# Attention decode on one core: VectorE weights seven of V's eight chunks instead of five, a group's sum stands behind the next scores, and x and the biases come in one transfer

## The chip, the cores and the metric

The kernel runs on one core of a Trainium2 chip. The metric is device time in microseconds (us) of one execution; the number that counts is the median of repeated runs.

## The reference

Two blocks alternate, twice each, on one token of width 512. All numbers are 32-bit floats.

```
x = x + A(layernorm(x))      # A: q = x@wq, 32 heads; scores = q.k * 128**-0.5; softmax;
x = x + B(layernorm(x))      #    o = p.v; out = o@wo      (k_cache, v_cache: 32 heads x 4096 x 128)
x = x + A(layernorm(x))      # B: gelu(x@w1 + b1)@w2 + b2  (w1 512x1376, w2 1376x512)
x = x + B(layernorm(x))
```

The caches are 64 MB each and are needed by both A blocks, so nearly all the bytes that move are K and V, read twice. Nothing is large in arithmetic: one query row per head.

## The kernel before

**The work in groups.** The 32 heads form G = 8 groups of 4 heads (J = 4). A group's K and V are 8 MB each, laid out as 128 partitions x 16384 columns, in C = 8 chunks of NC = 2048 columns; its wq and wo slices are together 2 MB ("the pair", 128 x 4096). The first A block goes through groups 0 to 7, the second through 7 down to 0 (it keeps a little of group 6 and 7 on chip). Between them runs the MLP, block B, and at the end a second MLP.

**Memory.** One large tile, `arena`, holds three homes of 64 KB a partition (A, B, C) that K and V take in turns (`RING`, line 37; `homes`, line 514), and the small areas SHARED, SCRATCH and PAIR behind. K of group g+2 comes into the home of V of group g; V of g+1 into that of K of g. There is one PAIR area. PSUM tiles: `pS` takes the scores, and the next queries while no scores are there; `pO` takes V's weighted sums, output products and transposed weights.

**The order of transfers.** All large loads are issued from SyncE (SPq, line 107) in program order: K of a group, V of it, its pair, K of the next, and so on. An issue waits until its destination was read for the last time. The pair of a group waits for the output product of the group before it (that reads the wo half of PAIR, line 402); K and V behind it in the queue then follow at once.

**A group on the engines** (functions `group`, `partly`, `weighted`, `sum_up`, `head`, `out_product`, `next_queries`):

- TensorE: with the group's K there, 32 matmuls give the scores into `pS` (`scores`, line 223, 64 records in the trace). `exponentials` (line 228) takes the maximum on VectorE, exp on ScalarE. `weights` (line 241) turns the weights on TensorE, and copies them out of `pO` on VectorE (line 246): these are needed before anything is done with V.
- V's chunks are shared: BY_PE = 3 of the 8 chunks are weighted by TensorE (`values`, line 255), the other five by VectorE, in place: one multiply of 128 x 10240 (line 266), then three adds that halve what is left (line 271: 4096, 2048, 2048 columns).
- While VectorE does this, TensorE makes the next group's queries into `pS` from the wq half of the pair (`next_queries`, line 380). VectorE turns them (four transposes, line 170), makes `z` (line 219) and clears `pS` (line 385). The next scores need `z` and the cleared `pS`.
- `sum_up` (line 275) adds VectorE's chunk into `pO`, `head` (line 279) turns it and reduces it to the group's output column, and `out_product` (line 299) multiplies it with wo. Of this, `sum_up` and `head` stand ahead of the next group's scores, `out_product` stands behind them.

The last group of the first A block, the one before it, and the last group of the second block have all eight chunks weighted by TensorE; the first groups of the second block, taken from what was kept, too. So eleven groups use VectorE's way. In the last group of all, V comes in pieces (4, 2, 1, 1 chunks), behind it wo, w1 and w2 of the closing MLP; `idle` (line 187) issues matmuls into an unused PSUM range while V's last chunks are worked on.

**The start.** x, b1 and b2 come by three small transfers that ScalarE issues (lines 130 to 132).

Of the kernel before, what the change touches and what calls it, by code (L numbers as in the profile page):

```python
# [17 lines left out]
P = 128  # L18
# [4 lines left out]
J = 4  # L23
# [15 lines left out]
KEPT_V = 26 * U  # L39
SHARED = B_AT + KEPT_V  # L40
SCRATCH = SHARED + 10 * U
PAIR = SHARED + 11 * U
KEPT_K = PAIR + 2 * NC
TURNED = SHARED + 9 * U
ARENA = KEPT_K + 2 * U
HALVES = ((0, 4), (4, 8))
BY_PE = 3
ZQ = C - 1 + J * C
WIDE = 32 * J + 8 + 3 + 1
FRONT = 192  # L50
# [5 lines left out]


@with_exitstack
def decode_layers(ctx: ExitStack, tc: tile.TileContext, x, k, v, w, w1, b1, w2, b2, out):
    nc = tc.nc  # L60
    const = ctx.enter_context(tc.tile_pool(name="const", bufs=1))
    psum = ctx.enter_context(tc.tile_pool(name="psum", bufs=1, space=bass.MemoryType.PSUM))
# [19 lines left out]
    def small(name, n=1):  # L82
        nonlocal first_front, rest
        if name.startswith("gelu_"):
            i = "huaztg".index(name[-1])
            return cells[:, gelu + FB * i : gelu + FB * (i + 1)]
        if name not in places:
            fit = [j for j in range(J) if gaps[j] + n <= ends[j]]
            if name in ("b1c", "b2c", "xcol"):
                places[name] = front, first_front, n  # L90
                first_front += n
            elif fit:
                places[name] = cells, gaps[fit[0]], n
                gaps[fit[0]] += n
            else:
                places[name] = cells, rest, n
                rest += n
        t, a, m = places[name]
        assert m == n and first_front <= FRONT and rest <= CELLS
        return t[:, a : a + n]  # L100

    def at(first, n):
        return arena[:, first : first + n]
# [9 lines left out]
    def quarters(first):  # L113
        return [at(first + U * j, U) for j in range(4)]
# [4 lines left out]
    def of_w(row, i, n):  # L119
        return w[row][:, NC * i : NC * (i + n)]  # L120
# [5 lines left out]
    wq_t = by_four(load(SHARED, of_w(1, 0, 1)))  # L126
    nc.vector.memset(wide, 1.0)
    nc.vector.memset(cells[:, WIDE:], 0.0)
    b1c, b2c, xcol = small("b1c", FB), small("b2c", 4), small("xcol", 4)
    nc.scalar.dma_start(xcol, x)  # L130
    nc.scalar.dma_start(b1c, b1)
    nc.scalar.dma_start(b2c, b2)

    make_identity(nc, ident)
    negmean = small("negmean")
# [19 lines left out]
    def of_32(t, n, i=0):  # L155
        return t[:, : 32 * n].rearrange("p (c q) -> p c q", q=32)[:, :, i]
# [59 lines left out]
    def queries(src, negm, wide=False, to=None):  # L216
        qt = turned(src, wide, to)
        z = zq
        nc.vector.scalar_tensor_tensor(z[:, C - 1 :].rearrange("p (j n) -> p j n", j=J)[:, :, 0], of_32(qt, J, 1), negm, of_32(qt, J),
                                       op0=ALU.mult, op1=ALU.add)  # L220
        return z

    def scores(z, c, kt):
        for j in range(J):
            matmul(pS[32 * j : 32 * j + C, :], z[:, C * j + C - 1 - c : C * j + 2 * C - 1 - c], kt[j],
                   start=(c == 0), stop=(c == C - 1))
# [32 lines left out]

    def weighted(pt, home):
        first = home + NC * BY_PE
        t = at(first, NC * (C - BY_PE)).rearrange("p (n d) -> p n d", d=P)
        w = pt.rearrange("p c j b -> p (c j b)")[:, 4 * J * BY_PE :]
        nc.vector.tensor_tensor(t, t, w.unsqueeze(2).to_broadcast([P, 4 * J * (C - BY_PE), P]), op=ALU.mult)  # L266
        n = C - BY_PE
        while n > 1:
            m = n // 2
            a, b = at(first + NC * (n - 2 * m), NC * m), at(first + NC * (n - m), NC * m)  # L270
            nc.vector.tensor_tensor(a, a, b, op=ALU.add)  # L271
            n -= m
        return quarters(first)

    def sum_up(t):
        for j in range(J):
            matmul(pO[32 * j : 32 * j + 4, :], one.to_broadcast([P, 4]), t[j], start=False, stop=True)

    def head(rl, last=False):
        ot = at(SCRATCH, U)  # L280
        nc.vector.transpose(ot, pO)  # L281
        o, on = small("o", 4), on_wide
        own = at(SCRATCH, 4 * 129).rearrange("p (b q) -> p b q", q=129)[:, :, :P]
        own = own.rearrange("p b (d q) -> p d b q", q=32)[:, :, :, 0]
        nc.vector.tensor_reduce(o, own, axis=AX.X, op=ALU.add)
        if last:
            nc.vector.tensor_scalar(on[:, :4], o, rl, None, op0=ALU.mult)
        else:
            nc.vector.tensor_scalar(in_quarters(on, 4), o.unsqueeze(1).to_broadcast([P, J, 4]), rl, None,
                                    op0=ALU.mult)  # L290
        return on
# [7 lines left out]
    def out_product(on, wt, to, narrow=False):  # L299
        for d in range(4):  # L300
            if narrow:
                for j in range(J):
                    matmul(to[32 * j : 32 * j + 1, :P], on[:, d : d + 1], wt[:, d, P * j : P * (j + 1)],
                           start=(d == 0), stop=(d == 3))
            else:
                matmul(to, on[:, d : d + P], wt[:, d, :], start=(d == 0), stop=(d == 3))
# [73 lines left out]
    def next_queries(xs, negm, wt, to=pO):  # L380
        for c in range(4):
            wide_query_block(to, c, xs, wt)
        z = queries(to, negm, wide=True)
        if to is pS:
            nc.vector.memset(pS, 0.0)  # L385
        return z

    def add_up(acc, own):
        t = small("acc", 4)
        nc.vector.scalar_tensor_tensor(t, own, 1.0, acc, op0=ALU.mult, op1=ALU.add)  # L390
        return t


    def group(z, acc, ahead, k_blocks):
        if ahead:
            t, rl, wt = ahead
            sum_up(t)
            on = head(rl)
        for c, t in k_blocks:
            scores(z, c, t)  # L400
        if ahead:
            out_product(on, wt, pO)
        p = exponentials(sc, nsc)
        if ahead:
            acc = add_up(acc, of_32(turned(pO, wide=True), 4))
        return acc, *weights(p)

    def partly(pt, v_blocks, home):
        for c, t in v_blocks:
            if c < BY_PE:  # L410
                values(c, pt, t, c)
        return weighted(pt, home)


    negm, z, sc, nsc = first_queries(xs, s, wq_t, wide=True)
# [2 lines left out]
    for g in range(G):  # L418
        final = g == G - 1
        k_home, v_home = RING[2 * g % 3], RING[(2 * g + 1) % 3]  # L420
        acc, pt, rl = group(z, acc, ahead, blocks(k, g, k_home, HALVES if final else ((0, C),)))
        ahead = None
        if g == G - 2:
            nc.scalar.copy(at(KEPT_K, 2 * U), at(k_home + NC * C - 2 * U, 2 * U))
        if g < G - 2:
            t = partly(pt, blocks(v, g, v_home), v_home)
            pair = load(PAIR, of_w(g % 2, g, 2))
            ahead = t, rl, by_four(pair[:, :NC])
            z = next_queries(xs, negm, by_four(pair[:, NC:]), to=pS)
            continue  # L430
        for c, t in blocks(v, g, v_home, LAST if final else ((0, C),)):
            values(c, pt, t, c)
            if final and c in (5, 7):
                idle(pS)
            if g == G - 2:
                for j in range(J):
                    i = 4 * c + j - KEPT_V // U
                    if i >= 0:
                        nc.scalar.copy(pK[i], t[j])
        if final:  # L440
            wo_t = by_four(load(PAIR, of_w(g % 2, g, 1)))
# [73 lines left out]
    for n in range(2, G):  # L515
        g, final = G - 1 - n, n == G - 1
        k_home, v_home = homes[(2 * n - 1) % 3], homes[2 * n % 3]
        acc, pt, rl = group(z, acc, ahead, blocks(k, g, k_home, HALVES if final else ((0, C),)))
        if not final:
            t = partly(pt, blocks(v, g, v_home, ((0, 6), (6, 8)) if n == 2 else ((0, C),)), v_home)  # L520
            pair = load(PAIR, of_w(g % 2, g - 1, 2))
            ahead = t, rl, by_four(pair[:, NC:])
            z = next_queries(xs, negm, by_four(pair[:, :NC]), to=pS)
            continue
        for c, t in blocks(v, g, v_home, LAST):
            values(c, pt, t, c)
            if c in (5, 7):
                idle(pS)
        wo_t = by_four(load(PAIR, of_w(g % 2, g, 1)))
        for a, b in W1_AT_END:  # L530
            load_w1(A_AT, a, b)
        for a, b in W2_AT_END:
            load_w2(A_AT + 11 * U, a, b)
        own = head_out(rl, wo_t, last=True)
# [47 lines left out]
```

## Time and profile before

| | |
|---|---|
| median of 3 runs | 673.45 us (673.1 to 673.54) |
| profiled execution, its own time | 673.82 us |
| its span (first to last instruction) | 672.0 us |
| TensorE matmul busy | 395.3 us (59%) |
| VectorE busy | 329.0 us (49%) |
| ScalarE, GpSimd busy | 22.8 us, 4.8 us |
| moved | 285.98 MB, 426 GB/s over the span |
| mean granted TensorE clock | 0.790 of full speed |

The profile gives busy times by engine, a strip of 40 slices over the span, the DMA queues, the chain of waits that ended last, and groups of instructions by line and form. A row of the timeline reads: start, duration, engine, line, operation, what it writes <- what it reads, form, count, and in brackets how long the engine was idle before it and what released it. "SPq" rows are SyncE's issues. A float matmul leaves two records, so 32 matmuls of scores are "x64". In the timeline of a later kernel the lines are that kernel's own; the added lines move them by 1 to 8.

### The profile page before, as it was taken

The page shows a single profiled execution, that of the slowest core. Times are in us where ns is not written, and L with a number is a line of the kernel's source. Part 1 is how long each engine was busy: PE and PEld are TensorE (multiplying, and loading weights), DVE is VectorE, ACT ScalarE, POOL GpSimd, SP SyncE. Part 2 cuts the span into 40 slices and gives each one's busy share as a digit, 9 for nine tenths or more (in the row PEclk, how much of TensorE's full clock was granted, in tenths as well). Part 3 has the DMA queues.
Part 4 walks back from the last instruction along what each step waited for, and adds up shares of the span by engine and source line. Part 5 has one row for each costly group of instructions (what it writes and reads, how often), then busy time and mean ns, then how long its engine had stood idle before and what let it go on. Part 6 is the DMA issues. An engine that isn't in the chain of part 4 may idle for free. (4 is left out here: it accounts for less than half of the span.)

```text
span 672.0 us, 5795 instructions
## 1 busy us (share of the span) xinstructions
PE 395.3 (59%) x2470; PEld 109.1 (16%) x2470; DVE 329.0 (49%) x480; ACT 22.8 (3%) x48; POOL 4.8 (1%) x23
## 2 busy tenths in 40 slices
PE   4533853647628456276777878728526566275586
PEld 1100210111102111011213222102101111021122
DVE  2049186293682845921112221492772936918522
ACT  0010000000000000011000110000000000000000
POOL 0000000000000000000000000000000000000000
PEclk9667775876768857787979999877759767677688
DMA  9999999999999999999999999999999999999996
GB/s 375 437 434 437 437 438 433 405 465 434 437 437 401 447 430 426 437 438 422 437 410 403 412 447 427 429 445 430 433 437 408 459 437 431 437 433 413 433 416 278
DMA packets 11545, 285.98 MB, mean 426 GB/s; under 512 B 1792, under 2 KB 1792, under 8 KB 3584
## 3 DMA queue, kind: packets, MB, share of 16 engines
q1 hardware_dynamic: 11088, 285.61, 99.0%
q8 instruction: 19, 0.31, 0.2%
q10 hardware_dynamic: 432, 0.01, 0.0%
q14 instruction: 6, 0.05, 0.0%
HBM read 285.62 MB, written 0.00 MB: 425 GB/s over the span
## 5 line engine op out<-in xcount | busy, mean ns | idle before, releaser
L111 PE MATMUL pO<-arena,cells 128*128 128x512 f32 (+4 forms) x376 | 92.9, 605 | 143.9 <-DVE arena L271 126.9
L111 PE MATMUL pS<-arena,front 128*8 128x512 f32 x1036 | 144.7, 699 | 34.8 <-DMA arena<-in_k 31.0
L266 DVE TENSOR_TENSOR arena<-arena 128x10240 f32<-128x10240 f32 x11 | 119.1, 10826 | 33.1 <-DMA arena<-in_v 30.2
L111 PE MATMUL pO<-arena 128*4 128x512 f32 x584 | 92.1, 786 | 45.8 <-DMA arena<-in_v 43.9
L271 DVE TENSOR_TENSOR arena<-arena 128x2048 f32<-128x2048 f32 (+1 forms) x33 | 98.5, 2985 | 0.7
L229 DVE TENSOR_REDUCE cells<-pS 128x1 f32<-128x512 f32 x16 | 11.1, 692 | 152.3 <-PE pS L111 152.3
L111 PEld LDWEIGHTS pO<-arena,cells 128*128 128x128 f32 (+3 forms) x376 | 28.2, 123 | 193.5 <-DVE arena L271 136.0
L111 PE MATMUL pS<-arena,cells 128*1 128x128 f32 (+1 forms) x328 | 50.0, 381 | 12.7 <-DMA arena<-in_w 10.1
L111 PEld LDWEIGHTS pS<-arena,front 128*8 128x8 f32 x1036 | 31.2, 101 | 154.3 <-issue 118.0
L281 DVE STREAM_TRANSPOSE arena<-pO 128x512 f32<-128x512 f32 x16 | 11.5, 717 | 55.1 <-PE pO L111 55.1
L243 PE MATMUL pO<-front,arena 128*128 128x128 f32 x64 | 12.3, 323 | 36.6 <-ACT arena L238 36.6
L111 PEld LDWEIGHTS pO<-arena 128*4 128x4 f32 x584 | 16.2, 101 | 108.2 <-issue 104.2
L170 DVE STREAM_TRANSPOSE arena<-pO 32x128 f32<-32x128 f32 x64 | 19.9, 311 | 20.0 <-PE pO L111 19.0
L111 PEld LDWEIGHTS pS<-arena,cells 128*1 128x1 f32 (+1 forms) x328 | 22.0, 117 | 46.8 <-issue 36.2
L238 ACT ACTIVATE arena<-pS,cells 128x512 f32<-128x512 f32 x16 | 12.4, 778 | 502.3 <-DVE cells L234 502.3
L232 DVE TENSOR_REDUCE cells<-cells 128x1 f32<-128x8 f32 x16 | 2.6, 161 | 29.4 <-PE pO L111 29.2
L243 PEld LDWEIGHTS pO<-front,arena 128*128 128x128 f32 x64 | 7.6, 155 | 49.7 <-ACT arena L238 48.5
L170 DVE STREAM_TRANSPOSE arena<-pS 32x128 f32<-32x128 f32 x44 | 13.7, 311 | 0.8
L172 DVE STREAM_TRANSPOSE arena<-pS 128x128 f32<-128x128 f32 x3 | 1.0, 317 | 12.1 <-PE pS L111 12.1
L248 DVE STREAM_TRANSPOSE cells<-cells 128x32 f32<-128x32 f32 x16 | 3.4, 214 | 6.7 <-ACT arena L238 5.5
L385 DVE MEMSET pS<- 128x512 f32 x11 | 5.3, 485 | 1.2
L111 PE MATMUL pO<-arena,front 128*128 128x128 f32 (+2 forms) x18 | 5.1, 385 | 0.0
(63 smaller groups left out, 72.9 us busy)
## 6 DMA issues: line engine op xcount, KB each, us to landing
arena<-in_w SPq DMA_DIRECT2D x13, 2048.0 KB, 11.4
arena<-in_k SPq DMA_DIRECT2D x4, 4096.0 KB, 25.0
arena<-in_v SPq DMA_DIRECT2D x2, 4096.0 KB, 38.9
arena<-in_w SPq DMA_DIRECT2D x6, 1024.0 KB, 20.1
arena<-in_v SPq DMA_DIRECT2D x3, 2048.0 KB, 42.6
arena<-in_v SPq DMA_DIRECT2D x1, 6144.0 KB, 30.3
arena<-in_w SPq DMA_DIRECT2D x6, 688.0 KB, 30.7
arena<-in_v SPq DMA_DIRECT2D x4, 1024.0 KB, 46.2
```

The source lines that it names most:

```text
L111: tc.keep_in_program_order(nc.tensor.matmul(*a, **kw))
L170: nc.vector.transpose(t[q], src[q, P * j : P * (j + 1)])
L172: nc.vector.transpose(t, src[:, :P])
L229: nc.vector.tensor_reduce(ml[:, 0:1], pS, axis=AX.X, op=ALU.max)
L232: nc.vector.tensor_reduce(m, mt[:, :C], axis=AX.X, op=ALU.max)
L238: nc.scalar.activation(p, pS, AF.Exp, bias=bias[:, 0:1], scale=sc, accum_out=ml[:, 0:1])
L243: tc.keep_in_program_order(nc.tensor.transpose(pT[:, b].rearrange("p j r -> p (j r)"), p[:, P * b : P * (b + 1)], ident))
L248: nc.vector.transpose(lt, ml)
L266: nc.vector.tensor_tensor(t, t, w.unsqueeze(2).to_broadcast([P, 4 * J * (C - BY_PE), P]), op=ALU.mult)
L271: nc.vector.tensor_tensor(a, a, b, op=ALU.add)
L281: nc.vector.transpose(ot, pO)
L385: nc.vector.memset(pS, 0.0)
```

## The change

Four edits are made.

1. BY_PE goes from 3 to 1: TensorE weights one of V's chunks, VectorE seven. The multiply is split into chunks 1 to 3 (128 x 6144) and 4 to 7 (128 x 8192), and the adds are of 6144, 4096 and 2048 columns.
2. The call that makes the next queries stands between the two multiplies (`between`), with the load of the pair ahead of it in the same function. The turned queries get an area of their own.
3. In `group`, the scores come first; `sum_up`, `head` and `out_product` of the group before come behind them, the latter two behind the maximum in `exponentials`. `head` gets an area of its own (TURNED_HEAD).
4. x, b1 and b2 are one array and one transfer of 128 x 19.

```diff
-BY_PE = 3
+BY_PE = 1
...
-    b1c, b2c, xcol = small("b1c", FB), small("b2c", 4), small("xcol", 4)
-    nc.scalar.dma_start(xcol, x)
-    nc.scalar.dma_start(b1c, b1)
-    nc.scalar.dma_start(b2c, b2)
+    by_dma = small("by_dma", FB + 8)
+    b1c, b2c, xcol = by_dma[:, :FB], by_dma[:, FB : FB + 4], by_dma[:, FB + 4 :]
+    nc.scalar.dma_start(by_dma, vectors)
...
-    def weighted(pt, home):
-        first = home + NC * BY_PE
-        t = at(first, NC * (C - BY_PE)).rearrange("p (n d) -> p n d", d=P)
-        w = pt.rearrange("p c j b -> p (c j b)")[:, 4 * J * BY_PE :]
-        nc.vector.tensor_tensor(t, t, w.unsqueeze(2).to_broadcast([P, 4 * J * (C - BY_PE), P]), op=ALU.mult)
-        n = C - BY_PE
+    def weighted(pt, home, between):
+        w = pt.rearrange("p c j b -> p (c j b)")
+
+        def times(a, b):
+            t = at(home + NC * a, NC * (b - a)).rearrange("p (n d) -> p n d", d=P)
+            q = w[:, 4 * J * a : 4 * J * b]
+            nc.vector.tensor_tensor(t, t, q.unsqueeze(2).to_broadcast([P, 4 * J * (b - a), P]), op=ALU.mult)
+
+        times(BY_PE, C // 2)
+        z = between()
+        times(C // 2, C)
+        first, n = home + NC * BY_PE, C - BY_PE
...
-        return quarters(first)
+        return quarters(first), z
...
     def group(z, acc, ahead, k_blocks):
+        for c, t in k_blocks:
+            scores(z, c, t)
         if ahead:
             t, rl, wt = ahead
             sum_up(t)
-            on = head(rl)
-        for c, t in k_blocks:
-            scores(z, c, t)
-        if ahead:
-            out_product(on, wt, pO)
         p = exponentials(sc, nsc)
         if ahead:
+            out_product(head(rl, to=TURNED_HEAD), wt, pO)
             acc = add_up(acc, of_32(turned(pO, wide=True), 4))
         return acc, *weights(p)
...
+            def queries_here():
+                load(PAIR, of_w(g % 2, g, 2))
+                return next_queries(xs, negm, by_four(at(PAIR + NC, NC)), to=pS)
+
+            t, z = partly(pt, blocks(v, g, v_home), v_home, queries_here)
+            ahead = t, rl, by_four(at(PAIR, NC))
```

On VectorE, from the multiply of V to the next group's maximum, for the last group that VectorE weights (line 266 is the multiply, 271 the adds, 170 the query transposes, 219 `z`, 385 the clearing of `pS`, 281 to 289 `head`, 229 the maximum), before:

```order
L266 TENSOR_TENSOR arena<-arena 128x10240
L271 TENSOR_TENSOR arena<-arena 128x4096
L170 STREAM_TRANSPOSE arena<-pS 32x128
L271 TENSOR_TENSOR arena<-arena 128x2048
L170 STREAM_TRANSPOSE arena<-pS 32x128
L271 TENSOR_TENSOR arena<-arena 128x2048
L170 STREAM_TRANSPOSE arena<-pS 32x128 x2
L219 SCALAR_TENSOR_TENSOR front<-arena,cells 128x4
L385 MEMSET pS 128x512
L281 STREAM_TRANSPOSE arena<-pO 128x512
L285 TENSOR_REDUCE cells<-arena 128x4
L289 TENSOR_SCALAR cells<-cells 128x4x4
```

and at the same place now (268 are the multiplies, 277 the adds, 391 the clearing, 229 and 231 the maximum and its turn, 287 the start of `head`):

```order
L268 TENSOR_TENSOR arena<-arena 128x6144
L268 TENSOR_TENSOR arena<-arena 128x8192
L170 STREAM_TRANSPOSE arena<-pS 32x128 x4
L277 TENSOR_TENSOR arena<-arena 128x6144
L219 SCALAR_TENSOR_TENSOR front<-arena,cells 128x4
L391 MEMSET pS 128x512
L277 TENSOR_TENSOR arena<-arena 128x4096
L277 TENSOR_TENSOR arena<-arena 128x2048
L229 TENSOR_REDUCE cells<-pS 128x1
L231 STREAM_TRANSPOSE cells<-cells 128x32
L287 STREAM_TRANSPOSE arena<-pO 128x512
```

The query transposes stand behind both multiplies (not between them, as the source is written), and `z` and the clearing stand behind the first and largest add. `head` moved from ahead of the maximum to behind it.

On TensorE, from V's chunks of that group to the turned weights of the last group (`pO<-arena 4x512` are V's chunks, `pS<-arena,cells 128x512` the next queries, `pO<-arena,cells 4x512` is `sum_up`, `pS<-arena,front 8x512` the scores, `pO<-arena,cells 128x512` the output product, line 243 the turned weights), before:

```order
L111 MATMUL pO<-arena 4x512 x12
L111 MATMUL pS<-arena,cells 128x512 x4
L111 MATMUL pO<-arena,cells 4x512 x4
L111 MATMUL pS<-arena,front 8x512 x32
L111 MATMUL pO<-arena,cells 128x512 x4
L243 MATMUL pO<-front,arena 128x128 x4
```

and now:

```order
L112 MATMUL pO<-arena 4x512 x4
L112 MATMUL pS<-arena,cells 128x512 x4
L112 MATMUL pS<-arena,front 8x512 x32
L112 MATMUL pO<-arena,cells 4x512 x4
L112 MATMUL pO<-arena,cells 128x512 x4
L243 MATMUL pO<-front,arena 128x128 x4
```

`sum_up` went from ahead of the scores to behind them; the output product directly follows it there. SyncE's order of transfers is the same in both.

More of the change, by code (lines that the diff above doesn't have):

```diff
@@ L41 @@
 SCRATCH = SHARED + 10 * U
+TURNED_HEAD = SHARED + 8 * U
 PAIR = SHARED + 11 * U
@@ L58, in decode_layers @@
 @with_exitstack
-def decode_layers(ctx: ExitStack, tc: tile.TileContext, x, k, v, w, w1, b1, w2, b2, out):
+def decode_layers(ctx: ExitStack, tc: tile.TileContext, vectors, k, v, w, w1, w2, out):
     nc = tc.nc
@@ L88, in small @@
             fit = [j for j in range(J) if gaps[j] + n <= ends[j]]
-            if name in ("b1c", "b2c", "xcol"):
+            if name == "by_dma":
                 places[name] = front, first_front, n
@@ L277, in sum_up, with head @@
             matmul(pO[32 * j : 32 * j + 4, :], one.to_broadcast([P, 4]), t[j], start=False, stop=True)
-    def head(rl, last=False):
-        ot = at(SCRATCH, U)
+    def head(rl, last=False, to=SCRATCH):
+        ot = at(to, U)
         nc.vector.transpose(ot, pO)
         o, on = small("o", 4), on_wide
-        own = at(SCRATCH, 4 * 129).rearrange("p (b q) -> p b q", q=129)[:, :, :P]
+        own = at(to, 4 * 129).rearrange("p (b q) -> p b q", q=129)[:, :, :P]
         own = own.rearrange("p b (d q) -> p d b q", q=32)[:, :, :, 0]
@@ L382, in next_queries @@
             wide_query_block(to, c, xs, wt)
-        z = queries(to, negm, wide=True)
+        z = queries(to, negm, wide=True, to=at(TURNED + P, P) if to is pS else None)
         if to is pS:
@@ L397, in group, with partly @@
             sum_up(t)
-            on = head(rl)
-        for c, t in k_blocks:
-            scores(z, c, t)
-        if ahead:
-            out_product(on, wt, pO)
         p = exponentials(sc, nsc)
         if ahead:
+            out_product(head(rl, to=TURNED_HEAD), wt, pO)
             acc = add_up(acc, of_32(turned(pO, wide=True), 4))
         return acc, *weights(p)
-    def partly(pt, v_blocks, home):
+    def partly(pt, v_blocks, home, between):
         for c, t in v_blocks:
@@ L411, in partly @@
                 values(c, pt, t, c)
-        return weighted(pt, home)
+        return weighted(pt, home, between)
     negm, z, sc, nsc = first_queries(xs, s, wq_t, wide=True)
@@ L425, in decode_layers @@
         if g < G - 2:
[L426 to L429, printed above, removed]
+            def queries_here():
[3 more added lines that the diff above has]
+            ahead = t, rl, by_four(at(PAIR, NC))
             continue
@@ L519, in decode_layers, with queries_here @@
         if not final:
[L520 to L523, printed above, removed]
+            def queries_here():
+                load(PAIR, of_w(g % 2, g - 1, 2))
+                return next_queries(xs, negm, by_four(at(PAIR, NC)), to=pS)
+            t, z = partly(pt, blocks(v, g, v_home, ((0, 6), (6, 8)) if n == 2 else ((0, C),)), v_home,
+                          queries_here)
+            ahead = t, rl, by_four(at(PAIR + NC, NC))
             continue
@@ L561 @@
     arrays = dict(
-        x=columns(a["x"])[:, :, 0],
+        vectors=np.concatenate((b1.reshape(J, FB, 32).transpose(0, 2, 1).reshape(P, FB),
+                                columns(a["b2"])[:, :, 0], columns(a["x"])[:, :, 0]), axis=1),
         k=apart(a["k"].reshape(G, J, C, U, DH).transpose(0, 4, 2, 1, 3).reshape(G, P, BLOCK)),
@@ L566 @@
         w1=columns(a["w1"]).reshape(P, 4 * J * FJ),
-        b1=b1.reshape(J, FB, 32).transpose(0, 2, 1).reshape(P, FB),
         w2=w2.reshape(J, FB, 32, D).transpose(0, 2, 1, 3).reshape(P, FB * D),
-        b2=columns(a["b2"])[:, :, 0],
     )
```

## Prediction

> **What bounds the kernel now.** I read the page first, then the busy time by stretch, the chain of waits, and the timeline of one middle group and of the last one.
>
> ```profile
> span 672.0 us, 5795 instructions
> q1 hardware_dynamic: 11088, 285.61, 99.0%
> q10 hardware_dynamic: 432, 0.01, 0.0%
> ```
>
> The big transfers (q1) take 99.0% of the time of all 16 DMA engines. In stretches:
>
> ```profile
> 1.00:666.30 665.30, 392.42 (x2414) 107.18 (x2414) 328.38 (x478) 22.84 (x48) 4.44 (x18) 0.79 1.00 430
> 89.80:112.00 22.20, 9.91 (x40) 2.24 (x40) 21.56 (x10) 0.00 (x0) 0.00 (x0) 0.73 1.06 456
> ```
>
> The columns are the stretch, its length, busy time of TensorE, weight loads, VectorE, ScalarE, GpSimd, the granted clock, the DMA share and GB/s. From 1 us to 666.3 us the DMA share is 1.00: no engine of the 16 has a gap worth naming. Where VectorE is busy throughout (21.56 of 22.20 us) the transfers are no slower. So compute is free as long as it gives buffers back in time, and it counts at the very end. The chain of waits says the same:
>
> ```profile
> 604.64 42.62 DMA arena<-in_v
> ...
> 647.32 18.94 DMA arena<-in_w
> ...
> 666.30 2.93 PE pS L111 x56
> ```
>
> The last w2 piece that TensorE waits for lands at 666.26 us; behind it is a tail of 5.7 us. Two questions follow: does the change ever let the queue run dry, and does it push the last group's compute beyond 666.3 us?
>
> **Transfers and the start.** Bytes on the big queue are the same. The three small transfers became one; q10, which carries them, rounds to 0.0% of the span, under 0.05% or 0.34 us, and two of three of its packets go: I take a gain of 0.2 us (ends 0 and 0.34). An x that lands earlier or later changes nothing, since the queue is full then.
>
> **Middle groups: does the queue run dry?** A middle group, from scores to V to the next scores, and the shortest issue-to-landing of the page:
>
> ```profile
> 113.95 8.58 PE L111 MATMUL pS<-arena,front 128*8 128x512 f32 x64 [1.90 <-DMA arena<-in_k]
> 122.46 3.70 PE L111 MATMUL pO<-arena,cells 128*128 128x512 f32 x8
> 126.19 0.33 SPq L107 DMA_DIRECT2D arena<-in_w  x1
> 133.22 10.83 DVE L266 TENSOR_TENSOR arena<-arena 128x10240 f32<-128x10240 f32 x1 [3.68 <-DMA arena<-in_v]
> 157.41 9.04 PE L111 MATMUL pS<-arena,front 128*8 128x512 f32 x64 [1.90 <-DMA arena<-in_k]
> out<-cells SPq DMA_DIRECT2D x1, 2.0 KB, 1.4
> ```
>
> The pair is issued when the output product is done (126.19), 3.66 us behind the end T of the scores (122.53). V, the only thing then left in the queue, is used at 133.22: the queue has 7.0 us in hand. VectorE gets V at 133.22 and the next scores start when K lands, 24.19 us later (157.41).
>
> VectorE's new work until the scores may start: from the multiply of 10240 columns (10.82 us) and the add of 4096 (4.42 us, quoted below) one column costs 1.042 ns and an instruction 0.16 us. So 6144 columns take 6.56 us, 8192 take 8.69. Multiplies 6.56 + 8.69, four transposes 1.29, add 6.56, `z` 0.23, clearing 0.48, and some 0.2 between them: 24.0 us. That is 0.2 us ahead of K: the scores start as before. The other adds (4.42 + 2.29) end at 30.9 us, the scores not before 24.2 + 8.5: `sum_up` finds them done.
>
> Behind T a chain is longer now. Rows for its parts, from the last group and two other places:
>
> ```profile
> 638.58 3.70 PE L111 MATMUL pO<-arena,cells 128*128 128x512 f32 x8
> 638.73 0.69 DVE L229 TENSOR_REDUCE cells<-pS 128x1 f32<-128x512 f32 x1 [6.48 <-PE pS L111]
> 639.45 0.21 DVE L231 STREAM_TRANSPOSE cells<-cells 128x32 f32<-128x32 f32 x1
> 631.05 0.72 DVE L281 STREAM_TRANSPOSE arena<-pO 128x512 f32<-128x512 f32 x1 [0.50 <-PE pO L111]
> 632.01 0.23 DVE L289 TENSOR_SCALAR cells<-cells 128x16 f32<-128x16 f32 x1
> 321.61 1.29 DVE L170 STREAM_TRANSPOSE arena<-pO 32x128 f32<-32x128 f32 x4 [3.79 <-PE pO L111]
> 644.41 0.66 PE L243 MATMUL pO<-front,arena 128*128 128x128 f32 x4 [2.13 <-ACT arena L238]
> 645.29 0.29 DVE L246 COPY arena<-pO 128x128 f32<-128x128 f32 x1
> 382.32 7.05 PE L111 MATMUL pO<-arena 128*4 128x512 f32 x64 [0.41 <-DVE arena L246]
> ```
>
> `sum_up` is 8 records; at full clock 64 take 7.05 us, so about 1.0 us, beside VectorE's maximum and its turn (T + 1.0). Then `head`, 1.19 us from 631.05 to 632.24, with two small operations between its parts (0.4): T + 2.65. The output product starts at T + 2.7 and ends at T + 6.4, where it was T + 3.66: the pair is issued 2.75 us later. Of 7.0 us in hand 4.3 are left; 1.4 us from issue to landing (for a small transfer on an idle queue) is my bound for what it needs, so nothing runs dry. The weights of V are ready at: T + 6.4, transposes 1.3 and 0.1, turned weights 0.66 beside five small VectorE steps (1.05), copy 0.29, in all T + 9.2; in the middle group 113.95 + 8.58 + 9.2 = 131.7, ahead of V at 133.2. So the middle costs nothing. The 88 matmuls fewer on TensorE are hidden as well.
>
> **The last group.** Here K waits for compute, not the other way round:
>
> ```profile
> 608.67 10.82 DVE L266 TENSOR_TENSOR arena<-arena 128x10240 f32<-128x10240 f32 x1 [2.40 <-DMA arena<-in_v]
> 619.53 4.42 DVE L271 TENSOR_TENSOR arena<-arena 128x4096 f32<-128x4096 f32 x1
> 626.72 2.29 DVE L271 TENSOR_TENSOR arena<-arena 128x2048 f32<-128x2048 f32 x1
> 630.06 0.48 DVE L385 MEMSET pS<- 128x512 f32 x1
> 630.73 7.92 PE L111 MATMUL pS<-arena,front 128*8 128x512 f32 x64
> 645.64 7.03 PE L111 MATMUL pO<-arena 128*4 128x512 f32 x48 [0.57 <-DVE arena L246]
> 655.62 0.72 DVE L281 STREAM_TRANSPOSE arena<-pO 128x512 f32<-128x512 f32 x1 [9.97 <-PE pO L111]
> 661.26 0.76 PE L111 MATMUL pO<-arena,cells 128*2 128x344 f32 x8 [0.41 <-DMA arena<-in_w]
> 664.24 1.05 PE L111 MATMUL pS<-arena,cells 128*1 128x128 f32 x32 [1.15 <-DVE cells L334]
> ```
>
> Now the scores start at 608.67 + 24.03 + 0.05 = 632.75 instead of 630.73. They took 7.92 us because `sum_up` just ahead of them (from 629.07) had used up part of the slow clock; now they start from rest. Two rows give the ends for that:
>
> ```profile
> 288.12 8.54 PE L111 MATMUL pS<-arena,front 128*8 128x512 f32 x64 [1.90 <-DMA arena<-in_k]
> 244.44 9.89 PE L111 MATMUL pS<-arena,front 128*8 128x512 f32 x64 [1.92 <-DMA arena<-in_k]
> ```
>
> I take 9.2, the middle. T = 641.95, V's weights are used at T + 9.23 = 651.2 instead of 645.64. From there to `head` it took 9.98 us, of which 1.7 are lost to a half clock:
>
> ```profile
> 642.74:646.15 3.41, 1.17 (x12) 0.61 (x16) 2.52 (x12) 0.87 (x2) 0.00 (x0) 1.00 0.98 420
> 646.15:649.56 3.41, 3.41 (x24) 0.69 (x20) 0.00 (x0) 0.00 (x0) 0.00 (x0) 0.50 1.00 420
> 663.21:666.63 3.42, 1.38 (x44) 1.04 (x48) 0.56 (x4) 0.21 (x1) 0.00 (x0) 1.00 0.87 350
> 666.63:670.04 3.41, 2.58 (x52) 1.60 (x40) 0.48 (x2) 0.00 (x0) 0.00 (x0) 0.50 0.07 28
> ```
>
> The clock is granted in windows of 3.41 us. A window in which TensorE was busy 1.17 us (34%) or 1.38 us (40%) is followed by one at 0.50. In the changed kernel the rest between the output product and V's chunks is T + 6.4 to T + 9.2, with 0.66 us of work in it: a window that holds all of it (starting at T + 5.8 to T + 6.4) is at most 1.26 us busy (37%), and with 0.1 us to either side still 40%. That is 0.8 of 3.41 us of possible starts, and where the windows lie I can't say. So about three times in four the clock stays: 9.98 − 1.7 = 8.3 us, and `head` starts at 659.5 instead of 655.62, 3.85 us later.
>
> The MLP behind waited 0.41 us for w1 (661.26) and 1.02 us for w2 (664.24 + 1.05 to 666.30); both have landed by then. So w2's matmuls start at 659.5 + (664.24 − 655.62) − 0.41 = 667.7. Before, 56 of their 88 records ran mostly at half clock (2.93 us); now TensorE has no long rest ahead of them, and 88 records take, at 32 in 1.05 us, 2.6 us: 670.25 instead of 669.23. **Sum:** +1.0 − 0.2 = +0.8 us. On the profiled execution's own 673.82 us that is 674.6; the median of the runs lies 0.37 lower: 674.2.
>
> The Trainium skill, "TensorE: Matmul & The Clock Gate", Part 1 and its section on HAM oscillation, has the clock fall after an idle window of about 3.4 us and asks for no rest longer than that. By that rule the rest of 2.8 us would never cost anything and the sum would stay at +0.8. The trace differs: the window from 642.74 was 34% busy, and the clock still fell. So the fall stays a case here, and by the page's word that the windows run free of the program, its phase isn't to be had from this trace.
>
> **Rivals.** (1) *The clock falls in the last group* (slower). A late window of clock also makes the scores long (9.6 to 9.9 us) and puts the next window's start on the rest: +0.4 to +0.7 from the scores, +1.7 from V's chunks, on top of +0.8: about 676.6. It decides when the window starts 5.7 to 6.5 us behind T. For it: it happened in the profiled execution, 646.15. Against: the rest is shorter now.
> (2) *The pair comes too late, and the queue runs dry* (slower). Price: what the delay exceeds 2.75 us by, less the margin of 4.3 − 1.4 = 2.9 us, ten times. It needs the output product at half clock (+3.7): then 0.8 us a pair, more where the scores are long, 8 to 12 us, 682 to 686. Against: TensorE rests only 1.7 us ahead of it, half of a window.
> (3) *The last group hides it all*: scores at 8.5 us or `z` a little earlier, and 0.4 more of slack: 673.3, the small transfers' 0.2 us less.
> (4) *Faster*: all of the last group's delay is hidden and the w2 tail, 2.93 us, runs at full clock (some 1.2 us less): 672.0. It needs `head` before 657, 2.5 us earlier than worked out.
>
> **How the numbers follow.** About 0.2% (1.35 us: below 672.1, above 674.8) is what a measurement of this kernel can tell from no change. Forecast +0.8 with its own ends of the scores (8.54 to 9.89: 673.5 to 674.9): 0.58. Rival 1: 0.22. Rival 2: 0.06. Rival 3: 0.10. Rival 4: 0.04. Slower is rivals 1 and 2 and a seventh of the forecast's own range, 0.36; faster 0.04; same the rest, 0.60. The range from 672.9 to 677.2 takes in rival 3 and rival 1 and leaves out rivals 2 and 4 and an edge.
>
> **What would show it.** In the changed profile: DMA share 1.00 until 666 us, the pair issued some 6.4 us behind the end of the scores, K and not VectorE releasing the scores in the middle groups, the last scores at about 632.7 and released by VectorE's clearing, V's last chunks from 651, and no wait for w2 in the tail. I am wrong if a DMA dip stands at each pair, if the multiplies take longer than their columns, or if the last group's scores start by 631.

## The result and the profile after

The changed kernel takes 682.09 us (median of 6 runs, 680.29 to 685.54); the kernel before took 673.5 us on the same chip (6 runs, 673.1 to 673.84). The ratio is 1.0133, 95% interval [1.0115, 1.0151]: 8.6 us slower. The forecast of 674.2 us and its range up to 677.2 are missed. What happened is what rival 2 names, the pair that comes too late; it had 0.06. The runs also spread over 5 us where the kernel before spreads over less than 1. The profiled execution took 683.58 us, its span 681.8 us, 9.8 us more than before.

The page of the changed kernel, span and big queue:

```profile
span 681.8 us, 5432 instructions
q1 hardware_dynamic: 11088, 285.61, 98.1%
```

Packets and bytes are those of before; their time is 98.1% of the span, not 99.0%, so transfers have gaps now. And 98.1% of 681.8 us is 668.8 us, where 99.0% of 672.0 was 665.3: the same packets also took some 3.5 us longer. Where, the busy time by stretch shows; first before (last number: GB/s):

```profile
1.00:660.00 659.00, 388.70 (x2356) 105.86 (x2356) 326.63 (x470) 22.63 (x47) 3.90 (x17) 0.79 1.00 430
100.00:300.00 200.00, 109.25 (x544) 27.72 (x544) 119.70 (x131) 4.52 (x9) 0.00 (x0) 0.74 1.00 432
300.00:320.00 20.00, 12.20 (x74) 3.24 (x74) 4.08 (x17) 4.05 (x8) 0.00 (x0) 0.83 0.98 424
320.00:380.00 60.00, 46.65 (x476) 15.81 (x478) 12.48 (x57) 1.25 (x4) 2.27 (x9) 0.94 0.99 411
470.00:490.00 20.00, 10.06 (x38) 2.61 (x36) 15.61 (x16) 0.87 (x2) 0.00 (x0) 0.81 1.00 430
490.00:640.00 150.00, 84.10 (x424) 21.23 (x425) 90.67 (x101) 2.60 (x6) 0.00 (x0) 0.73 1.00 432
```

and the same stretches now:

```profile
1.00:660.00 659.00, 361.58 (x2068) 105.30 (x2072) 414.76 (x471) 22.62 (x47) 3.69 (x16) 0.77 0.99 424
100.00:300.00 200.00, 98.67 (x474) 27.27 (x472) 158.91 (x131) 4.52 (x9) 0.00 (x0) 0.73 1.00 430
300.00:320.00 20.00, 14.42 (x80) 3.71 (x76) 4.77 (x20) 4.05 (x8) 0.00 (x0) 0.83 0.94 391
320.00:380.00 60.00, 45.88 (x438) 15.47 (x442) 11.52 (x55) 1.08 (x3) 2.27 (x9) 0.94 0.98 403
470.00:490.00 20.00, 12.99 (x80) 3.74 (x70) 9.94 (x20) 0.87 (x2) 0.00 (x0) 0.93 0.79 325
490.00:640.00 150.00, 70.38 (x308) 20.50 (x307) 122.05 (x99) 2.60 (x6) 0.00 (x0) 0.72 1.00 428
```

As an estimate, a stretch loses its length times (1 − GB/s now / GB/s before). Up to 660 us: 659 x (1 − 424/430) = 9.2 us, nearly all of the 9.8. By place: 0.9 us over the four pairs up to 300, 1.6 at the pair of 305, 1.2 in the MLP, 4.9 between 470 and 490, 1.4 over the three pairs behind (a GB/s is rounded, and a packet counts in the stretch in which it starts, so each is good to about half a us).

A middle group of the changed kernel, the one whose rows the prediction shows of before:

```profile
113.39 8.89 PE L112 MATMUL pS<-arena,front 128*8 128x512 f32 x64 [12.69 <-DMA arena<-in_k]
122.10 1.04 PE L112 MATMUL pO<-arena,cells 128*4 128x512 f32 x8
124.47 3.70 PE L112 MATMUL pO<-arena,cells 128*128 128x512 f32 x8 [1.33 <-DVE cells L295]
128.20 0.33 SPq L108 DMA_DIRECT2D arena<-in_w  x1
132.68 15.16 DVE L268 TENSOR_TENSOR arena<-arena 128x6144 f32<-128x6144 f32 x2 [2.00 <-DMA arena<-in_v]
```

K still releases the scores. Behind their end (122.28) come `sum_up`, `head`, the output product, and 5.92 us behind it the pair, where it was 3.66: 2.3 us later. From the pair's issue to the use of V are 4.5 us, where there were 7.0. This distance is called the pair's lead below.

The group with the large loss is the first of the second block that VectorE weights. The timeline of VectorE, then of TensorE and SyncE, and behind it two stretches of 2 us:

```profile
438.22 15.16 DVE L268 TENSOR_TENSOR arena<-arena 128x6144 f32<-128x6144 f32 x2
453.42 6.56 DVE L277 TENSOR_TENSOR arena<-arena 128x6144 f32<-128x6144 f32 x1
459.89 1.28 DVE L170 STREAM_TRANSPOSE arena<-pS 32x128 f32<-32x128 f32 x4
461.21 4.43 DVE L277 TENSOR_TENSOR arena<-arena 128x4096 f32<-128x4096 f32 x1
465.55 0.22 DVE L219 SCALAR_TENSOR_TENSOR front<-arena,cells 128x4 f32<-128x4 f32 x1
465.88 0.48 DVE L391 MEMSET pS<- 128x512 f32 x1
...
466.42 9.86 PE L112 MATMUL pS<-arena,front 128*8 128x512 f32 x64 [17.59 <-DVE pS L391]
482.21 0.33 SPq L108 DMA_DIRECT2D arena<-in_w  x1
```

```profile
478.00:480.00 2.00, 1.52 (x4) 0.81 (x5) 0.75 (x5) 0.87 (x2) 0.00 (x0) 1.00 0.00 0
480.00:482.00 2.00, 2.00 (x6) 0.63 (x4) 0.00 (x0) 0.00 (x0) 0.00 (x0) 1.00 0.00 0
```

Here, unlike in the group whose order stands under "The change", the add of 4096 columns (4.43 us) stands ahead of `z` and the clearing. The scores wait for the clearing, take 9.86 us, and the pair is issued at 482.21, behind V's landing: from 478 to 482 us no packet starts. The trace's packet records have V's last packets end at 477.9 to 480.3, engine by engine, and the pair's first one start at 483.17.

The last group:

```profile
616.79 15.16 DVE L268 TENSOR_TENSOR arena<-arena 128x6144 f32<-128x6144 f32 x2 [1.75 <-DMA arena<-in_v]
640.52 9.85 PE L112 MATMUL pS<-arena,front 128*8 128x512 f32 x64 [12.78 <-DVE pS L391]
658.86 5.33 PE L112 MATMUL pO<-arena 128*4 128x512 f32 x48 [0.46 <-DVE arena L246]
676.56 1.05 PE L112 MATMUL pS<-arena,cells 128*1 128x128 f32 x32 [0.41 <-DMA arena<-in_w]
677.80 1.03 PE L112 MATMUL pS<-arena,cells 128*1 128x128 f32 x24 [0.19 <-DMA arena<-in_w]
```

From VectorE's multiply to the scores are 23.73 us, and the end still waits for pieces of w2: in this run the late queue hides the last group's longer chain.

### The profile page after: what moved, and what is told of

It reads as the page before. It is cut to its first block, busy times and chain, and to the rows that moved or that the text cites. A ratio compares the mean times of both kernels' runs of the same rounds, so it can differ in the third digit from the quotient of the medians.

```text
span 681.8 us, 5432 instructions
## 1 busy us (share of the span) xinstructions
PE 377.8 (55%) x2294; PEld 110.8 (16%) x2294; DVE 419.2 (61%) x491; ACT 22.8 (3%) x48; POOL 4.8 (1%) x23
## 3 DMA queue, kind: packets, MB, share of 16 engines
q1 hardware_dynamic: 11088, 285.61, 98.1%
## 5 line engine op out<-in xcount | busy, mean ns | idle before, releaser
L268 DVE TENSOR_TENSOR arena<-arena 128x6144 f32<-128x6144 f32 (+1 forms) x22 | 166.8, 7621 | 21.6 <-DMA arena<-in_v 21.6
L277 DVE TENSOR_TENSOR arena<-arena 128x6144 f32<-128x6144 f32 (+2 forms) x33 | 145.8, 4420 | 0.7
L112 PE MATMUL pO<-arena,cells 128*128 128x512 f32 (+4 forms) x376 | 83.4, 501 | 31.2 <-DVE cells L295 16.0
L112 PE MATMUL pS<-arena,cells 128*1 128x128 f32 (+1 forms) x328 | 71.9, 437 | 39.6 <-DMA arena<-in_w 37.1
L112 PE MATMUL pO<-arena 128*4 128x512 f32 x408 | 63.1, 759 | 32.8 <-DMA arena<-in_v 30.6
L112 PEld LDWEIGHTS pS<-arena,cells 128*1 128x1 f32 (+1 forms) x328 | 29.6, 139 | 93.0 <-DMA arena<-in_w 49.0
L243 PE MATMUL pO<-front,arena 128*128 128x128 f32 x64 | 10.6, 291 | 29.4 <-DVE arena L170 16.2
L112 PEld LDWEIGHTS pO<-arena 128*4 128x4 f32 x408 | 9.8, 92 | 66.3 <-issue 61.9
```

Of the source, the lines that this page charges most:

```text
L112: tc.keep_in_program_order(nc.tensor.matmul(*a, **kw))
L243: tc.keep_in_program_order(nc.tensor.transpose(pT[:, b].rearrange("p j r -> p (j r)"), p[:, P * b : P * (b + 1)], ident))
L268: nc.vector.tensor_tensor(t, t, q.unsqueeze(2).to_broadcast([P, 4 * J * (b - a), P]), op=ALU.mult)
```

## The experiments

The theory (A): the pair comes late, its lead is short or gone, and the big queue loses time at each pair. Rivals: VectorE's larger share (B), TensorE's smaller share with its clock (C), and, raised later, that two smaller loads are better in themselves (D). Each kernel stands against the kernel before on the same chip; GB/s is that of 1 to 660 us.

| kernel | median us (runs) | ratio, 95% interval | GB/s |
|---|---|---|---|
| changed kernel | 682.09 (6) | 1.0133 [1.0115, 1.0151] | 424 |
| a_pin | 681.17 (6) | 1.0107 [1.0085, 1.013] | 426 |
| a_split | 676.58 (8) | 1.0045 [1.003, 1.006] | 429 |
| a_pin_split | 674.43 (12) | 1.0011 [0.9998, 1.0024] | 429 |
| a_three_pe | 680.04 (6) | 1.0106 [1.0083, 1.0129] | 426 |
| b_one_vec | 673.41 (11) | 0.9993 [0.9985, 1.0002] | 430 |
| b_pe1 | 702.23 (4) | 1.0424 [1.0408, 1.0439] | 414 |
| b_rest8 | 677.25 (7) | 1.0066 [1.0042, 1.0091] | 428 |
| b_rest16 | 685.52 (6) | 1.0192 [1.0168, 1.0215] | 424 |
| b_rest24 | 699.42 (6) | 1.0382 [1.0354, 1.041] | 413 |
| b_split | 674.26 (11) | 1.0009 [1.0, 1.0018] | 430 |
| b_rest16_split | 676.64 (6) | 1.005 [1.0033, 1.0067] | 428 |

Names with a_ start from the changed kernel, those with b_ from the one before, which took 673.62, 673.77, 673.44 and 673.72 us in the four sets.

**a_pin: the adds of 4096 and 2048 columns held behind the clearing in every group.**

```diff
-            nc.vector.memset(pS, 0.0)
+            cleared[0] = nc.vector.memset(pS, 0.0)
...
-            nc.vector.tensor_tensor(a, a, b, op=ALU.add)
+            added = nc.vector.tensor_tensor(a, a, b, op=ALU.add)
+            if n < C - BY_PE:
+                tc.add_manual_dep(added.ins, cleared[0].ins.name, mybir.DependencyInfo(
+                    mybir.DependencyClass.NoSync, mybir.DependencyReason.DATA), reason="order")
```

> The changed kernel, with VectorE's order fixed in one point: the adds of 4096 and 2048 columns come behind z and the clearing of pS in every group (in the changed kernel the first group of the second block has the 4096 add ahead of them). Theory A (two losses: that order in one group, 4.5 us of dry queue, and at each pair a queue with too little in hand, 3 to 4 us over all pairs): 677 to 678.5. Theory B (VectorE's seven chunks themselves are too long, in all groups alike): 680 or more. Theory C (fewer matmuls, so a lower granted clock on everything behind): unchanged, 682.

681.17 us: the size was missed. TensorE in the group of the large loss, the pair, and two stretches:

```profile
462.32 9.29 PE L112 MATMUL pS<-arena,front 128*8 128x512 f32 x64 [13.95 <-DMA arena<-in_k]
477.52 0.33 SPq L108 DMA_DIRECT2D arena<-in_w  x1
```

```profile
100.00:300.00 200.00, 97.67 (x460) 27.28 (x464) 158.28 (x130) 4.52 (x9) 0.00 (x0) 0.72 1.00 426
470.00:490.00 20.00, 12.24 (x48) 3.93 (x41) 13.08 (x21) 0.87 (x2) 0.00 (x0) 0.76 1.00 426
```

The order does what it should: K releases the scores, the pair comes 4.7 us earlier, and the dry stretch is gone (426 GB/s instead of 325). But the four pairs up to 300 us, whose issue this edit leaves alone, lose 200 x (1 − 426/432) = 2.8 us here, where they lost 0.9 in the profiled run of the changed kernel. So the dry stretch is no more than a part, and what a short lead costs differed between these two runs.

**a_split: the pair in two loads, the wq half first.** That half's place was read last by the next queries of the group before, long ago; only the wo half waits for the output product.

```diff
-                load(PAIR, of_w(g % 2, g, 2))
+                load(PAIR + NC, of_w(g % 2, g + 1, 1))
+                load(PAIR, of_w(g % 2, g, 1))
...
-                load(PAIR, of_w(g % 2, g - 1, 2))
+                load(PAIR, of_w(g % 2, g - 1, 1))
+                load(PAIR + NC, of_w(g % 2, g, 1))
```

> The changed kernel, with the pair loaded in two transfers: the wq half first, whose place is free long before, and the wo half behind it, which waits for the output product as the whole pair did. So 2.4 us more transfer lies in the queue when the issue that waits comes. VectorE's order is that of the changed kernel. Theory A: the pairs lose nothing any more (3 to 4 us) and the dry 4.5 us in the second block's first group shrink by about 2.4: 675.5 to 677. Theories B and C: unchanged, 681 to 683.

676.58 us: two thirds of the loss are gone, as A has it. No instruction of an engine's work changed; 1 MB (2.4 us at 430 GB/s) is queued ahead of the late point, and the lead is longer by that.

**a_pin_split: both.**

> Both: VectorE's adds pinned behind z and the clearing, and the pair in two transfers. Theory A: both losses gone, 673.5 to 675. Theory B: 680 or more. Theory C: 682.

674.43 us, 1.0011 [0.9998, 1.0024]: the loss is gone, and nothing is won. TensorE in the last group:

```profile
633.25 8.58 PE L112 MATMUL pS<-arena,front 128*8 128x512 f32 x64 [15.68 <-DVE pS L396]
650.32 5.33 PE L112 MATMUL pO<-arena 128*4 128x512 f32 x48 [0.46 <-DVE arena L246]
666.56 2.91 PE L112 MATMUL pS<-arena,cells 128*1 128x128 f32 x88 [1.10 <-DVE cells L345]
```

With the queue full, it is the kernel that the prediction had worked out: the scores start at 633.25 (632.75 worked out), V's last chunks at 650.32 (651.2), w2's matmuls wait for compute and no longer for their transfer, and the span is 672.5 us, 0.5 more than before (0.8 worked out).

**a_three_pe: the changed kernel with TensorE's three chunks back.**

```diff
-BY_PE = 1
+BY_PE = 3
```

> The changed kernel with BY_PE = 3 again: VectorE has five chunks, TensorE three; the queries, the sum behind the scores and the one transfer stay as changed. z then comes some 20 us behind V, ahead of K in all groups. Theory A: the loss in the second block's first group goes, that at the pairs stays, since their issue still stands behind the sum: 676 to 678.5. Theory B (VectorE's share): back at 673.5. Theory C (TensorE's share): back at 673.5.

680.04 us: three quarters of the loss (6.4 us) stay with the old shares, and with a mean granted clock of 0.794 (0.790 before, 0.776 changed). Both B and C had it back at 673.5, so neither is the main cause; what the shares have in the last quarter isn't told apart. A's own range, up to 678.5, is passed too. What is left of the change here, above all the place of the sum behind the scores, costs most of the 8.6 us.

**b_one_vec: edit 4 alone on the kernel before (the three small transfers in one).**

> The kernel before with only the one transfer for x, b1 and b2. All theories: 673.2 to 673.5, at most 0.3 us gained.

0.9993 [0.9985, 1.0002]: at most 1 us, and not told from nothing.

**b_pe1: seven chunks on VectorE, the sum ahead of the scores as before.**

```diff
-BY_PE = 3
+BY_PE = 1
```

> The kernel before with BY_PE = 1 alone: VectorE has seven chunks in one multiply of 14336 columns, and the sum stays ahead of the scores. The sum then waits for VectorE until 30 us behind V, the scores start some 7 us behind K, the pair is issued some 7 us later, when the queue is just empty. Theories A and B: 10 groups lose 3 to 6 us each, 700 to 735.

702.23 us, 4.24% slower. A middle group:

```profile
119.43 1.89 PE L111 MATMUL pO<-arena,cells 128*4 128x512 f32 x8 [19.52 <-DVE arena L271]
...
121.10 9.04 PE L111 MATMUL pS<-arena,front 128*8 128x512 f32 x64
```

`sum_up` waits for VectorE's three adds, and the scores, behind it, start at 121.10 instead of 113.95. So in the changed kernel the move of the sum is what makes seven chunks bearable, and itself costs what this case is about.

**b_late4 and b_late8: 4 or 8 calls of `idle` ahead of the output product.**

```diff
+            for _ in range(4):
+                idle(pO)
             out_product(on, wt, pO)
```

> The kernel before with four idle matmuls of 512 columns ahead of each output product, about 2.1 us, so that the pair is issued 2.1 us later and nothing else in the middle of a group changes much (the weights of V are ready 2.1 us later, still about ahead of V). It measures what the lead of the pair is worth by itself. By my prediction's bound (1.4 us are enough) no middle group loses: 673.5 to 674. Theory A (leads under some 5 us ahead of V's use cost time): a few tenths a pair, 674.5 to 676.

> The same with eight idle matmuls, about 4.2 us: leads of 1.5 to 2.8 us ahead of V's use. By my prediction's bound: 673.5 to 675. Theory A: one to two us at each of ten pairs, 680 to 692.

732.28 and 758.08 us, 1.086 [1.0844, 1.0875] and 1.1257 [1.1238, 1.1276]. They don't tell what they were made for: `idle` reads columns of home C, so a transfer into that home now waits for it. The stretch in b_late4:

```profile
112.00:130.00 18.00, 15.61 (x81) 4.50 (x78) 2.41 (x6) 0.00 (x0) 0.00 (x0) 0.79 0.16 55
```

55 GB/s for 18 us: a new dependency, not a shorter lead. The next three use matmuls that read nothing of a home.

**b_rest8, b_rest16, b_rest24: the kernel before with 8, 16 or 24 idle matmuls on constants ahead of the output product.** Shares, order of the sum and the rest stay; only what follows the idle matmuls comes later, the output product and the pair above all.

```diff
+            for _ in range(8):
+                matmul(pO[:, :P], zero[:, 0:1].to_broadcast([P, P]), ident, start=True, stop=True)
             out_product(on, wt, pO)
```

> The kernel before with 8 matmuls of 128 columns on constants (the identity, zero weights) ahead of each output product: they read nothing that is loaded later, and only make the output product, and so the pair's issue, later, by about 1.1 us. Lead of the pair (issue to VectorE's use of V) then 4.7 to 6 us. Theory A (the pair needs several us of lead): 673.5 to 674.5. My prediction's bound (1.4 us are enough): 673.6.

> The same with 16, about 2.2 us: leads of 3.6 to 4.9 us, about those of the changed kernel. VectorE's and TensorE's shares, the place of the sum and the order are those of before. Theory A: 676 to 680, most of the changed kernel's loss. My prediction's bound: 673.6. If the loss were VectorE's share or the place of the sum as such: 673.6.

> The same with 24, about 3.3 us: leads of 2.5 to 3.8 us. Theory A: 682 to 692, growing by about the delay itself from here on, ten times. My prediction's bound: 673.6 to 675.

The middle group of b_rest16:

```profile
122.56 3.84 PE L111 MATMUL pO<-front 128*128 128x128 f32 x32
126.23 3.60 PE L111 MATMUL pO<-arena,cells 128*128 128x512 f32 x8
129.87 0.33 SPq L107 DMA_DIRECT2D arena<-in_w  x1
134.61 10.82 DVE L266 TENSOR_TENSOR arena<-arena 128x10240 f32<-128x10240 f32 x1 [1.40 <-DMA arena<-in_v]
```

The pair and the use of V in the same group of b_rest8:

```profile
128.13 0.33 SPq L107 DMA_DIRECT2D arena<-in_w  x1
133.15 10.82 DVE L266 TENSOR_TENSOR arena<-arena 128x10240 f32<-128x10240 f32 x1 [1.68 <-DMA arena<-in_v]
```

A matmul took 0.23 to 0.26 us, more than the expectations have: the output product was 1.9, 3.7 and 5.5 us later. The price is 3.8, 12.1 and 26.0 us, above A's ranges in all three; put against the delays that came, 3.8 is in A's range for 2.2 us and 12.1 in that for 3.3 us. So a delay of the output product does it with the old shares and the old place of the sum. It makes V's weights late as well: in b_rest16 VectorE's start on V is no longer released by V in five of the eleven groups, in b_rest24 in nine. The next pair of runs tells that apart for b_rest16. The changed kernel's delay of 2.3 us lies between the first two; a straight line between them gives 5.5 us of its 8.6 as an estimate, and its own stretches without the dry one and the MLP 0.9 + 1.6 + 1.4 = 3.9. The price grows faster than the delay.

**b_split and b_rest16_split: the pair in two loads on the kernel before, and on b_rest16.**

```diff
-            pair = load(PAIR, of_w(g % 2, g, 2))
-            ahead = t, rl, by_four(pair[:, :NC])
-            z = next_queries(xs, negm, by_four(pair[:, NC:]), to=pS)
+            wq_t = by_four(load(PAIR + NC, of_w(g % 2, g + 1, 1)))
+            ahead = t, rl, by_four(load(PAIR, of_w(g % 2, g, 1)))
+            z = next_queries(xs, negm, wq_t, to=pS)
```

In the second block likewise.

> The kernel before, with the pair in two loads (the wq half first, which waits for nothing late, then the wo half). Theory A (the loss is the short lead of the pair): here the lead was enough already, so 673.0 to 674.2, the same as before. Rival D (two smaller loads are better in themselves, and the gain of the same edit in the changed kernel says nothing of the lead): faster by about the 0.9% that it gave there, 667 to 669.

> The kernel before with the 16 idle matmuls ahead of the output product, which alone made it 685.5, and the pair in two loads. Theory A: the wq half, 1 MB, is queued ahead of the late point and gives 2.4 us more of lead, so of the 3.7 us of delay 1.3 are left; 1.9 us cost 3.8, so 674 to 677. If something else in the delay costs (TensorE's work, V's weights that come later), the split changes little: 683 to 686. Rival D: 0.9% less than 685.5, 679 to 680.

Where the lead is long, the split gains nothing (1.0009 [1.0, 1.0018]); where it was made short, 1.0192 falls to 1.005, inside what A expects. D falls. The group of b_rest16_split:

```profile
122.56 3.84 PE L111 MATMUL pO<-front 128*128 128x128 f32 x32
129.86 0.33 SPq L107 DMA_DIRECT2D arena<-in_w  x1
133.49 10.82 DVE L266 TENSOR_TENSOR arena<-arena 128x10240 f32<-128x10240 f32 x1 [0.28 <-DMA arena<-in_v]
```

TensorE and the issue (now of the wo half) stand where they stood in b_rest16, and V lands 1.1 us earlier, in this group alone: the output product and V's weights are as late as in b_rest16, and only what is queued ahead differs. So about 9 of the 12.1 us are the pair's.

**What the packet records of these traces add.** They hold every DMA packet: a row of 16 KB of the pair for one of the 128 partitions, a row of 64 KB of K or V. The table has ten pairs, the six issued from 80 to 310 us and the four from 470 to 620; both losses are sums over the ten of the mean over the sixteen engines, the first from 6 us ahead of an issue to 8 us behind it.

| kernel | first packet of the pair behind its issue | without a packet around the ten issues | pairs' packets, longer than before | span, longer than before |
|---|---|---|---|---|
| before | 2.5 to 4.8 us | 0.2 us | 0 | 0 |
| changed kernel | 1.0 to 3.5 | 5.4 (4.5 at the dry stretch) | 3.4 | 9.8 |
| a_pin | 1.0 to 2.3 | 1.8 | 5.2 | 7.6 |
| a_three_pe | 1.3 to 2.2 | 1.4 | 4.2 | 5.9 |
| b_rest8 | 1.3 to 3.5 | 0.9 | 2.1 | 3.1 |
| b_rest16 | 1.0 to 2.7 | 4.3 | 4.1 | 10.8 |

Before, the engines go from V to the pair without a gap, and each of the pair's packets takes 0.61 us. In the others the first engine is through with V sooner behind the issue, some engines stand still, and the first sixteen packets of a pair take up to 1.40 us in the mean. Where the queue is empty, as at 482.21, the first packet follows the issue by 0.96 us. Packets of K and V take 2.42 us in all of them. The two losses together are most of the longer span in each. They also show why a_pin gains so little: the gaps shrink by 3.6 us, but the pairs' packets take 1.8 us longer.

## Why the prediction was wrong

- **What bounds the kernel**: right. The queue is full up to 666 us, and the loss is the queue's.
- **The small transfers** (−0.2): within b_one_vec's interval.
- **VectorE's work up to the scores** (24.0 us): right, 23.73 in the last group, and K releases the scores at 113.39. But it was worked out from one group's order and taken for all. In the first such group of the second block the built order puts a further 4.43 us ahead of `z`. The stretch around it lost 4.9 us in the profiled run; a_pin removes the dry queue, and the ratio falls only from 1.0133 to 1.0107, intervals overlapping.
- **The pair 2.75 us later**: 2.26, so even a little less than worked out.
- **"Of 7.0 us in hand 4.3 are left; 1.4 us from issue to landing (for a small transfer on an idle queue) is my bound for what it needs, so nothing runs dry"**: this is the step that failed, on both sides. The 7.0 us are those of one group, and others have less, down to 5.8 (83.99 to 89.78). They are counted to VectorE's use of V, which waits for the last of the sixteen engines. In the packet records of the kernel before, the first engine is through with V 2.2 to 3.3 us ahead of that use, and only 2.5 to 4.8 us behind the pair's issue; with 2.75 us taken off, −0.3 to 2.0 us are left. The 1.4 us belong to 2 KB that are stored at the very end on an idle queue, and say nothing of 2 MB that must follow on sixteen engines without a gap: at every pair of the table whose first packet starts less than 2 us behind the issue, the packets take longer, by 0.1 to 0.9 us in all. No view of the profile shows this, so the price should have stood open from zero up. b_rest8 has a delay of 1.9 us, under the forecast's own 2.75, and loses 3.8 us. The Trainium skill, "DMA: Bandwidth & Descriptors", "Anatomy of one DMA — SWDGE (gpsimd) path", puts the fixed part of a transfer that GpSimd issues at about 2 us. Taken over to these loads of SyncE, which is an estimate, it would have called a lead of 4.3 us enough as well; b_rest8 has leads of 4.1 to 6.3 us and loses all the same.
- **The last group** (+1.0): right in its mechanism, seen only when the queue is full again: a_pin_split's span is 0.5 us over that of before, in one profiled run each. In the changed kernel the late queue hides it.
- **Rival 1** (the clock falls in V's last chunks) did not come in the profiled run of the changed kernel: 48 records in 5.33 us instead of 7.03. It does come in a_split, with the same rest ahead of them:

```profile
645.26 3.70 PE L112 MATMUL pO<-arena,cells 128*128 128x512 f32 x8 [1.36 <-DVE cells L295]
650.43 0.63 PE L243 MATMUL pO<-front,arena 128*128 128x128 f32 x4 [1.47 <-DVE arena L170]
651.52 7.03 PE L112 MATMUL pO<-arena 128*4 128x512 f32 x48 [0.46 <-DVE arena L246]
```

So it stays a matter of where the window lies. In a_split the clock's window from 648.58 to 651.99 holds the rest, TensorE is busy 1.48 of its 3.41 us (43%), and the next window is at 0.50. In the changed kernel the window from 656.45 to 659.86 holds all but 0.2 us of it, is busy 1.63 us (48%), and the next stays at 1.00. The Trainium skill, "TensorE: Matmul & The Clock Gate", Part 1, has the clock fall after an idle window of some 3.4 us; here it falls behind one that is busy for 43%, a little more than the 40% that the prediction worked with. The rest between the output product and V's chunks is 2.6 us with 0.63 us of work in it.

- **Rival 2** had the right place, and its sum (682 to 686) holds the measured 682.09, but by luck: it asked for an output product at half clock, and that took 3.70 us as always, and about half of the profiled run's loss is one dry stretch that it doesn't have. It had 0.06 because the same 4.3 and 1.4 us stood in it as a margin.

What stays open: why a pair's first packets take longer when they start soon behind the issue, and why by different amounts (the four pairs up to 300 us took 1.2 us longer than before in the changed kernel, 2.5 in a_pin, with first packets 1.3 to 2.5 and 1.4 to 1.9 us behind the issue). How much of the median's 8.6 us is the one dry stretch isn't settled by medians either: some 5 us were lost there in the profiled run, but by the two ratios only about 1.8 are won where it is taken away.

## What to carry to other kernels

Where a full transfer queue sets the time, ask of each edit which issue it delays, and how much work is left in the queue then: for the engine that is through first, and in the group with the least. Here a lead that shrank had a price well before it was gone, and a latency measured on an idle queue didn't bound it. If one load waits for two readers, the part whose reader is early can go ahead as a load of its own. And look at the built order in every group, not in one: a scheduler need not place the same source the same way twice.

## What was not expected of the hardware

With leads of 4.1 to 6.3 us to the use of V (b_rest8) the queue already moves less: 428 GB/s instead of 430 from 1 to 660 us at 1.9 us of delay, then 424 at 3.7 and 413 at 5.5. Not all of it is gaps: the same 16 KB packets take longer in the packet records. And with short leads the time of a run scatters: 5.3 us between the fastest and slowest of 6 runs of the changed kernel, 7.0 of 7 runs of b_rest8, against 0.7 of 6 runs of the kernel before on the first chip and 1.5 to 3.7 of its 12 to 19 runs in the four sets.
